# The start of an attention and feed-forward kernel: other loads, other engines and another order for the first head block

## The chip, the cores and the metric

The kernel runs on one core of a Trainium2 chip. The metric is the device time of one execution in microseconds (us); the number that counts is the median of several runs. Beside it there is one profiled execution with a trace of every instruction. In the profile PE is TensorE (PEld its weight loads), DVE is VectorE, ACT is ScalarE, POOL is GpSimd and SP is SyncE. L330 is line 330 of the kernel before.

## The reference

For 8 batches of 8 heads with 576 positions and 64 channels the kernel computes causal attention with an additive bias, and then a gated feed-forward block over the 4608 tokens of width 512 (1536 hidden channels):

```
scores = q @ k.T / 8 ;  cum = cumsum(max(s, 0))
bias   = min(-(cum[query] - cum[key]), 0)
attn   = softmax(where(key > query, -1e9, scores + bias)) ;  x = attn @ v
out    = (silu(x @ w_gate) * (x @ w_val)) @ w_out
```

q, k, v, s and the weights come as float32, the output is float32. Inside, the kernel works in bfloat16 with float32 sums.

## The kernel before, in words

**Head blocks.** The 64 heads are worked on in 16 blocks of four. For each block k and q are loaded as tiles of 128 partitions (rawk, rawq), cast to bfloat16 (ck, cq), transposed on PE against an identity (through PSUM banks) and copied from PSUM into two tiles KQ[block % 2][r], r = 0 or 1. A KQ tile holds two heads: 64 of its 128 partitions are the 64 channels of k and q, and four rows of the other 64 partitions are the bias: the running sum of s, split into a high and a low part in bfloat16, beside constant rows of about 1 and -1, so that one matmul over the partitions gives scores and bias together. For r = 0 the channels are partitions 0 to 63 and the bias rows 64 to 67, for r = 1 the bias rows are 0 to 3 and the channels 64 to 127. All other rows must be zero, because the score matmul contracts over all 128 partitions.

**Scores.** `score_piece(bh, ci)` (L352) takes a PSUM bank, adds a mask from the tile `lower` in batch 0 (L367), multiplies (L373) and lets ACT exponentiate (L383), which gives the bank back. Four pieces make a head. `av_piece` (L410) multiplies the result with v, `av_out` (L426, L427) divides.

**Banks.** There are eight PSUM banks. `take` gives the bank that was released longest ago, by the order of the program. A bank that holds transposed k or q is given back only when `pe_out` (L328 on ACT, L330 on DVE) has copied both halves r out of it.

**Order.** The order on each engine is the order of the program, written out by hand (L949 to L1032); engines wait on each other through semaphores, and each engine works strictly through its list. The trace shows that the dependencies go by region and not by tile: PE reads the high part of the sums in HL from 6.77 us on (L914), while DVE still writes the low part (L245, to 6.93 us) and the copy (L246, 6.97 to 7.77 us).

**The start.** SP loads s and then k and q of block 0 in halves r (L145, from 1.45 us). PE runs 32 idle products to raise its clock (`keep_warm`, L900). DVE sets constants, scans s (L241), and writes the high and low sums into HL (L244, L245, L246). ACT casts the halves k and q of r = 0 (L268), PE transposes them (L315), and ACT and DVE copy them out (`row_out`, `pe_out`). The bias rows of head 0 are not loaded by DMA: PE picks them with a selection matrix (`pick`, L914), and ACT and DVE scale them into KQ (`picked_row`, L925, L929). The bias rows of heads 1 to 3 come by one DMA each from HL (`aug`, L188 on SP), when all of HL is written; those of block 1 follow on the same queue. POOL makes the identity and the mask, clears rows of KQ (L226, L234), loads k and q of block 1 (L145), casts the halves r = 1 of block 0 (L270), loads v of batch 0 (L162, five DMAs), casts q of block 1 (L260), loads weights (L346) and casts v (L173). DVE copies out the halves r = 1 of block 0 (L970, L972), casts k of block 1 (L971), and copies out block 1, first the halves r = 0 (`half_batch`, L989, L992) and, after the scores of head 3, the halves r = 1 (L996 to L998). Later blocks are worked on beside the feed-forward part, which fills PE.

## Time and profile before

| what | value |
|---|---|
| median of 3 runs | 373.54 us (373.49 to 373.61) |
| the profiled execution | 373.92 us, its span 372.0 us |
| PE busy | 363.2 us (98% of the span), 3288 matmuls |
| DVE, ACT, POOL busy | 291.1, 239.9, 212.4 us |
| PE busy from 5 to 19 us | 11.87 of 14 us |
| PE busy from 19 to 27 us | 8.00 of 8 us |
| the chain that ended last, shares | PE 83%, DVE 10%, DMA 2%, ACT 2%, issue 2%, POOL 1% |

The span is the time from the first to the last instruction of the profile. The chain is the list of instructions that a step-by-step walk back from the last instruction meets, each time to what released it. A share of busy time is a mean over stages: the kernel as a whole is filled with matmuls, its first 19 us are not.

### The profile page before, as it was taken

How to read it: one execution, taken by the hardware profiler on the slowest of the kernel's cores; microseconds unless marked ns; L12 is line 12 of the kernel's file. 1: busy time of each engine (PE TensorE's matmuls, PEld its weight loads, DVE VectorE, ACT ScalarE, POOL GpSimd, SP SyncE). 2: the span in 40 equal slices, each digit the busy share in tenths (PEclk: the TensorE clock that was granted, in tenths of full speed). 3: DMA queues.
4: the chain of work that ended last, by engine and by line, in shares of the span. 5: the costliest groups of instructions: out<-in, count | busy, mean ns of one | idle time of the engine just before them, and what ended most of it. 6: DMA issues, size and time to landing. Idle time of an engine off the chain costs nothing.

```text
span 372.0 us, 8786 instructions
## 1 busy us (share of the span) xinstructions
PE 363.2 (98%) x3288; PEld 230.3 (62%) x3288; DVE 291.1 (78%) x585; ACT 239.9 (65%) x470; POOL 212.4 (57%) x325
## 2 busy tenths in 40 slices
PE   7899999999999999999999999999999999999996
PEld 6684556655555557855685558655865585476465
DVE  8978776377985899589967897699868867975984
ACT  8877776778886967688757875786565523323321
POOL 8983556955266547594749464955675516315320
PEclk9999999999999999999999999999999999999999
DMA  7999999799879996996789484994142113002003
GB/s 238 220 254 259 215 272 257 239 299 227 252 172 307 199 268 181 162 285 217 214 179 263 160 185 157 265 210 114 40 121 62 35 30 118 0 3 86 28 0 113
DMA packets 97133, 64.21 MB, mean 173 GB/s; under 512 B 77228, under 2 KB 82724, under 8 KB 97092
## 3 DMA queue, kind: packets, MB, share of 16 engines
q1 hardware_dynamic: 84964, 41.46, 46.9%
q0 software_dynamic: 12128, 22.21, 22.7%
q8 instruction: 25, 0.41, 0.5%
q14 instruction: 16, 0.13, 0.1%
HBM read 37.90 MB, written 19.86 MB: 155 GB/s over the span
## 4 chain that ended last, share of the span: by engine, by line
PE 83%; DVE 10%; DMA 2%; ACT 2%; issue 2%; POOL 1%; DVEq 0%; ACTq 0%
PE banks L643 43%; PE banks L749 17%; PE banks L373 9%; PE banks L410 7%; PE banks L700 5%; DVE kq L330 3%; DMA pk<-ks 2%; DVE pp L666 2%; DVE ht L677 1%; DVE kq L288 1%; ACT th L664 1%; POOL vt L173 1%; ACT pt L383 1%; PE banks L459 1%; PE banks L301 0%
## 5 line engine op out<-in xcount | busy, mean ns | idle before, releaser
L383 ACT ACTIVATE pt<-banks 128x512 bf16<-128x512 f32 (+1 forms) x256 | 120.4, 511 | 29.8 <-PE banks L373 17.1
L643 PE MATMUL banks<-XT,wg 128*128 128x512 bf16 x432 | 111.4, 379 | 0.4 <-DVE pp L666 0.3
L643 PE MATMUL banks<-XT,wv 128*128 128x512 bf16 x432 | 110.9, 379 | 0.1
L664 ACT ACTIVATE th<-banks 128x512 bf16<-128x512 f32 x108 | 64.7, 599 | 56.3 <-PE banks L643 51.4
L666 DVE SCALAR_TENSOR_TENSOR pp<-th,banks 128x512 bf16<-128x512 bf16 x108 | 73.7, 682 | 18.3 <-ACT th L664 18.0
L677 DVE SCALAR_TENSOR_TENSOR ht<-pp,banks 128x512 bf16<-128x512 bf16 x108 | 74.1, 687 | 10.3
L373 PE MATMUL banks<-kq 128*128 128x128 bf16 (+4 forms) x576 | 76.4, 240 | 0.8 <-DVE kq L330 0.3
L686 POOL TENSOR_TENSOR ht<-ht 128x512 bf16<-128x512 bf16 x35 | 40.4, 1154 | 53.3 <-DVE su L684 53.2
L373 PEld LDWEIGHTS <-kq 128*128 128x128 bf16 x576 | 46.1, 98 | 30.7 <-issue 2.4
L643 PEld LDWEIGHTS <-wv 128*128 128x128 bf16 x432 | 38.4, 98 | 36.2 <-issue 0.2
L643 PEld LDWEIGHTS <-wg 128*128 128x128 bf16 x432 | 38.4, 98 | 34.1 <-issue 0.7
L410 PEld LDWEIGHTS <-pt 128*128 128x128 bf16 x960 | 41.8, 98 | 17.7 <-issue 0.7
L388 POOL TENSOR_SCALAR_AFFINE_SELECT pt<-pt 128x512 bf16<-128x512 bf16 x56 | 36.6, 653 | 25.9 <-ACT pt L383 21.7
L410 PE MATMUL banks<-vt,pt 128*128 128x65 bf16 x960 | 46.8, 194 | 0.5 <-DVE ot L427 0.4
L444 POOL DMA_DIRECT2D xs<-ot x24 | 21.7, 904 | 30.4 <-DVE ot L427 28.0
L749 PEld LDWEIGHTS <-ht 128*128 128x128 bf16 x336 | 31.2, 98 | 4.3
L427 DVE TENSOR_TENSOR ot<-banks,rc 128x320 bf16<-128x320 f32 x64 | 31.5, 492 | 2.2
L188 POOL DMA_DIRECT2D kq<-HL x48 | 29.2, 610 | 0.0
L700 PE MATMUL banks<-wo,ht 128*128 128x512 bf16 x96 | 25.8, 379 | 0.0
L749 PEld LDWEIGHTS <-su 128*128 128x128 bf16 x252 | 23.6, 98 | 3.3
L814 POOL TENSOR_TENSOR ysb<-ysb 128x512 f32<-128x512 f32 x12 | 15.2, 1269 | 15.3 <-DVE ysb L808 15.3
L749 PE MATMUL banks<-WS,ht 128*128 128x256 bf16 x168 | 22.9, 273 | 0.0
(101 smaller groups left out, 377.2 us busy)
## 6 DMA issues: line engine op xcount, KB each, us to landing
out_dram<-ysb POOLq DMA_DIRECT2D x32, 256.0 KB, 4.0
rawv<-in_v_dram SPq DMA_DIRECT2D x28, 256.0 KB
rawk<-in_k_dram SPq DMA_DIRECT2D x12, 576.0 KB
rawq<-in_q_dram SPq DMA_DIRECT2D x12, 576.0 KB
xs<-ot POOLq DMA_DIRECT2D x24, 160.0 KB, 3.7
ks<-ck SPq DMA_DIRECT2D x11, 288.0 KB
qs<-cq SPq DMA_DIRECT2D x11, 288.0 KB
rawk<-in_k_dram POOLq DMA_DIRECT2D x3, 576.0 KB, 6.0
```

What stands on the lines that cost most here:

```text
L373: nc.tensor.matmul(sc[:, o : o + w], T[:, 1, e * S + 128 * tj : e * S + 128 * (tj + 1)], T[:, 0, e * S + lo : e * S + hi], start=not maske ...
L383: nc.scalar.activation(pt[:, c0 : c0 + n], sc, AF.Exp, scale=0.125)
L388: nc.gpsimd.affine_select(pt[:, 1088:1600], pt[:, 1088:1600], pattern=[[0, 4], [1, 128]], compare_op=ALU.is_ge, fill=zreg, base=0, channel ...
L410: nc.tensor.matmul(av[:, bi * (D + 1) : (bi + 1) * (D + 1)], pt[:, c0 : c0 + 128], VT[b % 2][:, tj, h, :], start=(tj == 0), stop=(tj == bi),)
L427: nc.vector.tensor_mul(ot[:, :, e * D : (e + 1) * D], av3[:, :, 0:D], rc[:, :, None].to_broadcast([128, NCH, D]),)
L643: nc.tensor.matmul(view(bs, TT), w[:, c, f0 : f0 + 128], xt[:, c, :], start=(c == 0), stop=(c == 3),)
L664: nc.scalar.activation(th, pg, AF.Tanh, scale=0.5)
L666: nc.vector.scalar_tensor_tensor(pp, in0=th, scalar=1.0, in1=pg, op0=ALU.add, op1=ALU.mult)
L677: nc.vector.scalar_tensor_tensor(hp[:, 2 * k2 : 2 * k2 + 2, :].rearrange("p a n -> p (a n)"), in0=pp, scalar=0.5, in1=pv, op0=ALU.mult, op ...
L686: (nc.vector if ft == NFT - 1 else nc.gpsimd).tensor_sub(hp[:, 1:3, :], hp[:, 1:4:2, :], hp[:, 0:3:2, :])
L700: nc.tensor.matmul(view(pys[ts_], DM), hps[ft // 2][:, 2 * (ft % 2) + half, c0 : c0 + 128], WO[j][:, ft % WKO, :], start=(ft == 0), stop=( ...
L749: nc.tensor.matmul(ps, lhs(p), rhs(p), start=(first and p == 0), stop=(last and p == NP - 1), skip_group_check=True,)
```

## The change

The parts of the change, in the order of the program:

- k and q of block 0 are no longer loaded as float32 by SP. `load_first` loads each half by a DMA from POOL that casts to bfloat16 on the way, into a layout in which each half r is contiguous. The casts on ACT (L268) and POOL (L270) are gone. The mask `lower` is made between the halves r = 0 and r = 1; the loads of block 1 follow directly.
- A tile `idle`, set to zero by DVE, takes the place of the identity in the 31 (before: 32) idle products at the start. Ten more idle products stand between the third and the fourth score piece of head 0, on a bank of their own.
- The score matmul of r = 0 uses 68 partitions instead of 128. The zeroing of the other rows of the two r = 0 tiles (DVE L222 for the columns of head 1 in the first, POOL L234 in the second) is gone; `pads` clears only the padding columns of k, and that of the second pair of tiles comes later.
- The bias rows of heads 1 to 3 come in parts: the constant row by one DMA each before the sums exist (`aug_const`), and the sums by two DMAs each (`aug_sums`) that do not need the copy of the sums (L246). That copy, now `second_copy`, comes after `picked_row(0)` on DVE, and the bias rows of block 1 after it.
- `pick` is called in the order high part for k and q, then low part for k and q.
- The copy of k of r = 1 out of PSUM goes to ACT, one half before the first exponential and one after the third. The transposes of q of r = 1 come before the first score piece on PE. DVE casts k and also q of block 1, after the copies of q of r = 1.
- On POOL, the loads of v come before the copies and transposes of the rest; the cast of q of block 1 is gone from it.

```diff
@@ -110,6 +110,7 @@
     r_m = first.tile([128, 1], FP32)
     PTP = {0: first, "bufs": 7}
     lower = first.tile([128, 512], BF16)
+    idle = first.tile([128, 128], BF16)
 
     with tc.manual_schedule():
         loaded = {}
@@ -149,6 +150,24 @@
                 ),
             )
 
+        cts = {}
+        firsts = {}
+
+        def load_first(name, r):
+            if r == 0:
+                cts[name, 0] = cp.tile(
+                    [128, J, NR, D], BF16, tag="c" + name, bufs=2, name="c" + name
+                )
+                firsts[name] = cts[name, 0].rearrange("x j r d -> x (j r d)").rearrange(
+                    "x (r j d) -> x r j d", r=NR, j=J
+                )
+            nc.gpsimd.dma_start(
+                firsts[name][:, r].rearrange("x j d -> x (j d)"),
+                SRC[name][0][0, 2 * r : 2 * r + 2, :, :].rearrange(
+                    "e (p j) d -> (e p) (j d)", j=J
+                ),
+            )
+
         def load_qk(hb):
             load_one(hb, "k")
             load_one(hb, "q")
@@ -195,22 +214,26 @@
             nc.gpsimd.memset(VT[i][:, :, :, D : D + 1], 1.0)
             nc.gpsimd.memset(VT[i][64:128, 4, :, 0:D], 0.0)
 
-        for r in range(NR):
-            load_one(0, "k", (r, r + 1))
-            load_one(0, "q", (r, r + 1))
-
-        nc.vector.memset(warm, 0.0)
-        nc.vector.memset(one_s, 1.0)
-        nc.scalar.activation(warm, warm, AF.Exp)
-        nc.vector.memset(sel, 0.0)
-        nc.vector.memset(HL[:, 0:2, 0, :].bitcast(FP32), ONES2)
-        nc.vector.memset(HL[:, 2:4, 1, :].bitcast(FP32), NEGS2)
         make_identity(nc, ident)
+        load_first("k", 0)
+        load_first("q", 0)
         nc.gpsimd.memset(lower, 0.0)
         nc.gpsimd.affine_select(
             lower, lower, pattern=[[0, 4], [1, 128]],
             compare_op=ALU.is_ge, fill=nc.gpsimd.to_reg(MASKED), base=0, channel_multiplier=-1,
         )
+        load_first("k", 1)
+        load_first("q", 1)
+        for nm in ("k", "q"):
+            load_one(1, nm, eng=nc.gpsimd)
+
+        nc.vector.memset(warm, 0.0)
+        nc.vector.memset(one_s, 1.0)
+        nc.vector.memset(idle, 0.0)
+        nc.scalar.activation(warm, warm, AF.Exp)
+        nc.vector.memset(sel, 0.0)
+        nc.vector.memset(HL[:, 0:2, 0, :].bitcast(FP32), ONES2)
+        nc.vector.memset(HL[:, 2:4, 1, :].bitcast(FP32), NEGS2)
         for lo in range(2):
             nc.vector.tensor_copy(
                 sel[:, lo, 64 + lo : 68 : 2], ident[0:BH, 0:1].to_broadcast([BH, 2])
@@ -219,11 +242,10 @@
         nc.vector.tensor_add(r_k[up], ident[up, 64:65], ident[up, 65:66])
         nc.vector.tensor_add(r_q[up], ident[up, 66:67], ident[up, 67:68])
         nc.vector.tensor_scalar_mul(r_m[up], r_q[up], -1.0)
-        nc.vector.memset(aug_rows(0, 0)[:, :, S // 2 :], 0.0)
 
         def pads(i):
             for r in range(2):
-                nc.gpsimd.memset(KQ[i][r][64 * r : 64 * r + 64, :, NR * S :], 0.0)
+                nc.gpsimd.memset(KQ[i][r][64 * r :, 1, NR * S :], 0.0)
 
         for i in range(2):
             rows = aug_rows(i, 1)
@@ -231,11 +253,7 @@
                 rows.rearrange("p a n -> p (a n)"),
                 one_s[0:64, 0:1].to_broadcast([64, NR * S + 64]), 0.0,
             )
-        nc.gpsimd.memset(aug_rows(1, 0), 0.0)
         pads(0)
-        pads(1)
-        for nm in ("k", "q"):
-            load_one(1, nm, eng=nc.gpsimd)
 
         nc.vector.tensor_scalar(s_sb, s_sb, 0.0, 8.0, ALU.max, ALU.mult)
         nc.vector.tensor_tensor_scan(
@@ -243,12 +261,25 @@
         )
         nc.vector.tensor_copy(HL[:, 0, 1, :], c8)
         nc.vector.tensor_sub(HL[:, 1, 1, :], c8, HL[:, 0, 1, :])
-        nc.vector.tensor_copy(HL[:, 2:4, 0, :], HL[:, 0:2, 1, :])
+
+        def second_copy():
+            nc.vector.tensor_copy(HL[:, 2:4, 0, :], HL[:, 0:2, 1, :])
+
+        def aug_dst(h):
+            r, e = divmod(h, 2)
+            r0 = 64 * (1 - r)
+            return KQ[0][r][r0 : r0 + 4, :, e * S : (e + 1) * S]
+
+        def aug_const(h):
+            nc.sync.dma_start(aug_dst(h)[2:4, 1, :], HL[h : h + 1, 2:4, 1, :])
+
+        def aug_sums(h):
+            rows = aug_dst(h)
+            nc.sync.dma_start(rows[0:2, :, :], HL[h : h + 1, 0:2, :, :])
+            nc.sync.dma_start(rows[2:4, 0, :], HL[h : h + 1, 0:2, 1, :])
 
         SP4 = [nc.sync] * 4
         GP4 = [nc.gpsimd] * 4
-
-        cts = {}
 
         def cast_one(hb, name, eng):
             cts[name, hb] = cp.tile([128, J, NR, D], BF16, tag="c" + name, bufs=2, name="c" + name)
@@ -259,16 +290,6 @@
             else:
                 eng.tensor_copy(dst, src_t)
 
-        def cast_half(hb, name, r, eng):
-            if r == 0:
-                cts[name, hb] = cp.tile([128, J, NR, D], BF16, tag="c" + name, bufs=2, name="c" + name)
-            dst = cts[name, hb][:, :, r, :]
-            src_t = loaded[name, hb][:, r, :, :]
-            if eng is nc.scalar:
-                nc.scalar.copy(dst, src_t)
-            else:
-                eng.tensor_copy(dst, src_t)
-
         def scratch(hb):
             for name, SC in (("k", KS), ("q", QS)):
                 nc.sync.dma_start(
@@ -310,10 +331,9 @@
                 ps = view16(bs, (j1 - j0) * 128).rearrange("p (j x) -> p j x", x=128)
                 tps[name, g] = [ps, bs, 2]
             ps = tps[name, g][0]
-            ct = cts[name, hb]
             for j in range(j0, j1):
                 nc.tensor.transpose(
-                    ps[64 * r : 64 * r + 64, j - j0, :], ct[:, j, r, :], ident
+                    ps[64 * r : 64 * r + 64, j - j0, :], firsts[name][:, r, j, :], ident
                 )
 
         def pe_out(hb, name, g, r, eng):
@@ -358,7 +378,7 @@
                 )
             pt = pts[bh]
             r, e = divmod(hh, 2)
-            T = KQ[hb % 2][r]
+            T = KQ[hb % 2][r][0 : 68 if r == 0 else 128]
             bs = take()
             n = sum(hi - lo for _, lo, hi in CHUNKS[ci])
             sc = view(bs, n)
@@ -897,7 +917,7 @@
 
         def keep_warm(n, b):
             for _ in range(n):
-                nc.tensor.matmul(view(b, 128), ident, ident, start=True, stop=True)
+                nc.tensor.matmul(view(b, 128), idle, idle, start=True, stop=True)
 
         def row_half(nm, r):
             for g in range(2):
@@ -907,15 +927,14 @@
             for g in range(2):
                 pe_out(0, nm, g, r, engs[g])
 
-        def pick(side):
+        def pick(side, lo):
             b = PICK[side]
-            for lo in range(2):
-                for c0, c1 in ((0, 512), (512, S)):
-                    nc.tensor.matmul(
-                        banks[:, b + c0 // 512, 0 : c1 - c0], sel[:, lo, :],
-                        HL[:, lo, 1, c0:c1], start=(lo == 0), stop=(lo == 1),
-                        skip_group_check=True,
-                    )
+            for c0, c1 in ((0, 512), (512, S)):
+                nc.tensor.matmul(
+                    banks[:, b + c0 // 512, 0 : c1 - c0], sel[:, lo, :],
+                    HL[:, lo, 1, c0:c1], start=(lo == 0), stop=(lo == 1),
+                    skip_group_check=True,
+                )
 
         def picked_row(side):
             b = PICK[side]
@@ -946,35 +965,41 @@
                 av_piece(h, range(NCH))
                 av_out(h)
 
-        keep_warm(32, 7)
-        cast_half(0, "k", 0, nc.scalar)
-        cast_half(0, "q", 0, nc.scalar)
-        aug(0, SP4, range(1, HB))
-        aug(1, SP4)
+        keep_warm(31, 7)
+        for h in range(1, HB):
+            aug_const(h)
+        for h in range(1, HB):
+            aug_sums(h)
+        load_v(0, range(5), nc.gpsimd)
         row_half("k", 0)
         row_out("k", 0, nc.scalar, nc.scalar)
-        cast_half(0, "k", 1, nc.gpsimd)
-        cast_half(0, "q", 1, nc.gpsimd)
-        load_v(0, range(5), nc.gpsimd)
         row_half("q", 0)
-        pick(1)
-        pick(0)
-        pe_out(0, "q", 0, 0, nc.scalar)
-        pe_out(0, "q", 1, 0, nc.vector)
+        row_out("q", 0, nc.scalar, nc.vector)
+        for lo in range(2):
+            for kq in (1, 0):
+                pick(kq, lo)
         picked_row(1)
         picked_row(0)
+        second_copy()
+        aug(1, SP4)
         row_half("k", 1)
+        pe_out(0, "k", 0, 1, nc.scalar)
+        row_half("q", 1)
         score_piece(0, 0)
         score_piece(0, 1)
-        row_half("q", 1)
-        row_out("k", 1, nc.vector, nc.vector)
-        cast_one(1, "k", nc.vector)
         row_out("q", 1, nc.vector, nc.vector)
+        for nm in ("k", "q"):
+            cast_one(1, nm, nc.vector)
         score_piece(0, 2)
+        pe_out(0, "k", 1, 1, nc.scalar)
+        b = take()
+        for _ in range(10):
+            nc.tensor.matmul(view(b, 128), idle, idle, start=True, stop=True)
+        give(b)
         score_piece(0, 3)
-        cast_one(1, "q", nc.gpsimd)
         w_load("g", 0)
         init_vt(0)
+        pads(1)
         for c in range(3):
             cast_v(0, c, nc.gpsimd)
         load_one(2, "k", eng=nc.gpsimd)
```

## The prediction

> **What bounds the kernel now.** I read first the busy time by stretches, because a share over the whole span mixes stages. Columns: stretch, its length, then for each engine busy us (instructions), the granted clock, the DMA share and GB/s.
>
> ```profile
> 9.00:11.00 2.00, 1.87 (x21) 1.20 (x20) 1.97 (x4) 1.12 (x3) 2.00 (x4) 1.00 0.94 314
> 11.00:13.00 2.00, 1.36 (x16) 0.97 (x15) 1.97 (x3) 2.00 (x6) 2.00 (x3) 1.00 0.97 244
> ...
> 17.00:19.00 2.00, 1.63 (x20) 1.11 (x19) 1.97 (x4) 2.00 (x7) 2.00 (x4) 1.00 1.15 211
> 19.00:21.00 2.00, 2.00 (x49) 1.72 (x46) 1.58 (x5) 1.82 (x5) 2.00 (x4) 1.00 1.13 304
> ...
> 200.00:300.00 100.00, 100.00 (x928) 63.55 (x926) 82.61 (x173) 66.85 (x135) 61.96 (x93) 1.00 0.57 139
> ```
>
> PE (first pair) has gaps until 19 us and hardly any from 19 us on, while DVE is full until 19 us. All of the change lies before that point. Its worth is therefore the shift of the moment at which PE becomes the bound. Next the chain of waits up to there (start, length, what):
>
> ```profile
> 8.44 0.17 DVE kq L929
> 8.61 0.63 issue
> 9.24 1.20 DVE kq L330 x2
> 10.44 0.29 issue
> 10.73 0.76 DVE ck L260
> 11.49 0.03 issue
> 11.53 1.47 DVE kq L330 x2
> ...
> 15.96 2.83 DVE kq L330 x4
> 18.79 0.04 issue
> 18.83 0.19 PE banks L367
> ```
>
> DVE works without a break from the bias rows of head 0 (8.44) to the last copy of block 1 (18.79). That copy gives back the bank for the last score piece of head 5 (18.83); from there the chain is PE. ACT is the second limit:
>
> ```profile
> 9.80 3.46 ACT L383 ACTIVATE pt<-banks 128x512 bf16<-128x512 f32 x8 [0.98 <-PE banks L373]
> 13.91 6.45 ACT L383 ACTIVATE pt<-banks 128x512 bf16<-128x512 f32 x16 [0.65 <-PE banks L373]
> 20.54 1.69 ACT L383 ACTIVATE pt<-banks 128x512 bf16<-128x512 f32 x4 [0.18 <-PE banks L373]
> ```
>
> The exponentials of heads 0 to 5 fill 9.80 to 20.36, with 0.65 idle at 13.3. After 20.36 ACT waits for PE 0.18, and before head 7 another 0.2, so ACT may be about 0.4 us later, relative to PE, than it is now.
>
> **The loads, the unknown of this change.** SP's load of the first k half was issued at 1.45 and released ACT at 4.68: 3.2 us. POOL's load of k of block 1, twice the bytes, shows
>
> ```profile
> 4.85 0.91 POOL L145 DMA_DIRECT2D rawk<-in_k_dram  x1
> 5.75 0.74 POOL L145 DMA_DIRECT2D rawq<-in_q_dram  x1
> ```
>
> and 5.3 us to landing (q: 6.0). So a half-sized casting load from POOL costs between 3.2 and 5.3 us from the start of its issue. By the trace's packet records the first packet follows 1.6 us after the start of POOL's issue against 1.3 for SP's k half; the bytes of a half are the same as SP's and its queue is empty, so I stay near that row: 3.6 us. POOL's issues take 0.9 (first) and 0.75 each. After the identity (1.38) come k at 1.4, q at 2.3, the mask (0.52 + 0.63), then the r = 1 halves, k at 4.2 and q at 4.95, and block 1 at 5.7 and 6.45. Landings: k 5.0, q 5.9, k of r = 1 7.8, q of r = 1 8.55; block 1 by its own row 5.7 + 5.3 = 11.0 and at most 6.45 + 6.0 = 12.45.
>
> A row here speaks against POOL as the issuer. Of the v loads, with 0.88 us as the median, the one that lay beside DVE's cast of k (10.73 to 11.49, SBUF to SBUF) took 1.08. The Trainium skill (DMA: Bandwidth & Descriptors, section SWDGE vs HWDGE vs iDMA) says why that can be: POOL writes its descriptors into SBUF, and DVE locks it out there in its two-port modes, which loads from SP never meet. In the changed kernel the first issue lies beside DVE's two constant fills of HL (1.20 to 2.34). By the row this costs 0.2 us on the first load; if the rule meant a full lock, up to 0.9 us on the k half, and the sum below would lose about half of its gain.
>
> **The change part by part.**
>
> *k and q of r = 0.* Removed: two ACT casts of 0.67, which put the transposes at 5.40 and 6.15. Now they start at 5.0 and 5.9: 0.4 and 0.25 earlier, with bounds from 0.8 earlier to 1.4 later (3.2 and 5.3 in place of 3.6).
>
> *The sums on DVE.* The 0.59 of zeroing before the scan is gone, a small fill (0.06 to 0.17 by the other fills) is added. s landed at 3.51 by the trace's DMA records and was first used at 3.73, so 0.2 is gained, not 0.5: HL high 5.95 instead of 6.15, low 6.7 instead of 6.93. The copy L246 (0.80) leaves the path: the copy of q starts at 6.7 instead of 7.70.
>
> *Picks.* Four matmuls take 0.5 us (eight took 1.15 with the last one's tail). q's transposes end at 6.4, the high parts at 6.9, the low parts at 7.4, plus 0.2: 7.6 instead of 7.92. ACT's three copies (1.97) run from 5.5 to 7.5. Both `picked_row` steps start at 7.6 and end at 8.4 (ACT, 0.82) and 8.5 (DVE, 0.89; before: 9.33). DVE is 0.8 ahead here.
>
> *PE's order.* Both transposes of r = 1 now stand before the first score: 8.6 to 9.1 for q's nine (0.5 plus tail). Mask and scores of the first piece take 0.65: the first exponential starts at 9.75, before: 9.80. What was gained in front of it waits here for q of r = 1.
>
> *ACT.* Two copies of 0.75 and 0.72 are added (0.66 apart when they follow each other). The first lies between 8.4 and 9.1, where ACT waits for PE anyway; without that cover it would cost 0.66. The second is on ACT's path, and takes the place of the 0.65 of idle time at 13.3, which came from the copies of r = 1 (k and q both on DVE, to 13.0). Heads 0 to 5 thus end at 9.75 + 3.46 + 0.66 + 6.45 = 20.3, before: 20.36.
>
> *DVE.* After 8.5: the copy `second_copy` 0.8 (9.3), two copies of q 1.46 (10.8), the cast of k 0.79 (11.6; landed at 11.0), the cast of q, when it lands, 0.79: 12.4 to 13.2, most likely 12.4, since in the profile of before DVE's 10.73 cast did not wait and DMA has the same bytes ahead of it. Then eight copies of 0.725: 18.2, at worst 19.0. Before: 18.79. Moved off DVE: 1.46; onto it: 0.76 for q of block 1.
>
> *What hides at nothing.* The ten idle products (0.056 apart, 0.56) stand while PE waits for ACT's banks. The score matmuls with 68 instead of 128 partitions: half of the 576; the nearest rows are the weight load with 64 partitions (94 ns) against 98 with 128, and 64 x 512 products of 380 ns against 378; bounds 0 to -1 us over all, value 0. Bias rows: nine small DMAs on SP of 0.61; three lie before 6.7, six end at 10.4; head 1's two are issued by 7.9 and land some 2 us later, before its scores (10.9). Behind them on SP stand only the rows of block 1, needed from 16 us on. The `pads` of 0.20 to 0.42 and the v loads move on POOL: v starts at 7.65 instead of 8.25, and with the casts of POOL gone (0.92 + 0.89 + 1.16) the weights are issued about 0.9 earlier.
>
> *Sum.* DVE hands back the last bank 0.6 earlier; ACT, with its 0.4 of room, allows it. From there all is PE, so I pass it on, less 0.1 for what later waits on DMA: **0.5 us**. The profiled execution would go from 373.92 to 373.4; the median, 0.38 below it, from 373.54 to **373.0**.
>
> **The rivals.**
>
> *More gain.* The loads land as SP's do (3.2): q of r = 1 at 8.15, block 1 early, the first exponential at 9.3 or, with a shorter issue (0.61, the smallest row of POOL), 8.8. DVE and ACT then both end about 1.0 earlier: 372.5; with the bounds of the 68-partition scores, 372.2. For it: an empty queue, half the bytes. Against it: the 5.3 and 6.0 of POOL's own rows.
>
> *No net change.* q of block 1 lands at 12.2 or later; DVE waits for it with eight copies behind it, and ends as before: 373.5. For it: 6.45 + 6.0 = 12.45 by the row.
>
> *Slower.* q of r = 1 lands late and everything behind it in PE's list waits, though head 0 needs nothing of it. DVE's end is its landing plus 0.7 (transposes) plus 1.46 + 1.58 + 5.8, so it decides from 9.2 us on, 4.3 us after its issue; ACT's end (landing + 1.2 + 10.57) passes its room a little earlier. By POOL's 5.3 it lands at 10.25: 1.0 us later, 374.5. A clock that is granted later would add to it: the 32 idle products of before ran 107 ns apart, and 59 apart is what the transposes show at 5.4; an idle PE from 4.4 to 5.0 may cost some of it.
>
> **How the numbers follow.** Forecast 0.40 (372.6 to 373.3), more gain 0.22, no net change 0.15, slower 0.23. The range leaves out a tenth on each side: 372.2 to 374.4. A difference of 0.2%, 0.75 us, is about what a measurement of this kernel can tell from none. Of the forecast a quarter lies beyond it, with all of the second case: faster 0.32. Of the slower case 0.17 lies beyond. The rest is within: 0.51.
>
> **What would show it.** Right: transposes at 5.0 and 5.9, `picked_row` ending at 8.5, the first exponential near 9.75 right behind q's transposes, DVE's last copy of block 1 near 18.2, and PE without gaps from there. Wrong: ACT or PE waiting on q of r = 1 after 9.2, DVE waiting on rawq of block 1 after 12.2, transposes spaced 0.1 us, or the shift at 18 us lost again before the end.

## The result and the profile after

The kernel after takes **379.15 us** (median of six runs, 377.94 to 379.50), the kernel before 374.43 (six runs: the three ahead of the prediction, at 373.49 to 373.61, and three more, at 375.25 to 377.56): ratio 1.012, 95% interval 1.0091 to 1.0149. It is slower, and outside the range of the prediction. The profiled execution took 378.90 us with a span of 376.9, 4.9 above the span of before. The kernel before itself was found between 373.3 and 378.6 us in the runs beside the experiments, so a difference of a few tenths of a per cent is read below from its interval and from the traces, not from two medians.

By stretches, in the columns that the prediction explains:

```profile
9.00:11.00 2.00, 1.37 (x20) 1.09 (x18) 1.55 (x3) 1.59 (x4) 2.00 (x3) 1.00 1.00 330
11.00:13.00 2.00, 0.00 (x0) 0.00 (x0) 0.76 (x1) 0.69 (x1) 1.90 (x4) 1.00 0.99 286
13.00:15.00 2.00, 1.15 (x9) 0.84 (x10) 0.76 (x1) 0.54 (x2) 0.66 (x3) 0.79 1.06 227
15.00:17.00 2.00, 1.78 (x17) 1.60 (x16) 0.75 (x2) 1.38 (x4) 1.23 (x2) 0.50 1.14 187
```

The first pair is PE: from 11 to 13 us it does nothing, where before it was busy for 1.36 of these 2 us. DVE, full before, is busy for 0.76. The DMA share of that stretch is 0.99: PE and, for most of it, DVE stand still, the DMA engines do not. From 15 to 17 us PE looks busy, but at a granted clock of 0.50 (the third number from the end).

The chain of work that ended last names what PE waited for:

```profile
6.22 0.75 DVE HL L263
...
7.00 6.71 DMA kq<-HL
13.71 0.14 issue
13.85 0.19 PE banks L393
...
19.65 2.82 DVE kq L350 x4
...
22.51 0.19 PE banks L387
```

The low part of the sums ends at 6.97 us (L263). SP issues head 1's bias rows at 7.00, and they land 6.7 us later. The score piece that waits for them, 68 partitions by 64 columns (L393), is the last piece of **head 0**: its fifth key tile reaches 64 columns into head 1's half of KQ, so it needs head 1's rows. PE works strictly through its list, so all behind this piece waits too. The same piece in PE's row of before and of after (in brackets: the idle time in front, and what ended it):

```profile
10.79 0.19 PE L373 MATMUL banks<-kq 128*128 128x64 bf16 x1
```

```profile
13.85 0.19 PE L393 MATMUL banks<-kq 68*128 68x64 bf16 x1 [3.48 <-DMA kq<-HL]
```

The last two steps of the chain are the ones that the prediction's chain ended with, at 18.79 and 18.83 us before: 3.68 us later now. By the starts of the feed-forward activations the shift is 3.6 at 32 us, and 4.13 at the last store, so most of it happens in this place; the rest of the 4.9 of the span lies in a few smaller waits and 0.8 us in the last stores.

DVE's row in time, and ACT's, show that DVE waited for loads as well:

```profile
12.14 0.76 DVE L291 CAST ck<-rawk 128x1152 bf16<-128x1152 f32 x1 [1.56 <-DMA rawk<-in_k_dram]
13.75 0.76 DVE L291 CAST cq<-rawq 128x1152 bf16<-128x1152 f32 x1 [0.84 <-DMA rawq<-in_q_dram]
16.25 1.45 DVE L350 COPY kq<-banks 64x640 bf16<-64x640 bf16 x2 [1.74 <-PE banks L322]
```

```profile
9.38 1.58 ACT L403 ACTIVATE pt<-banks 128x512 bf16<-128x512 f32 x3 [0.39 <-PE banks L393]
14.08 0.22 ACT L403 ACTIVATE pt<-banks 128x64 bf16<-128x64 f32 x1 [2.38 <-PE banks L393]
```

The first exponential is 0.42 us earlier than before, at 9.38. What the change gained in front is thus there, and is lost right behind it. Last, why the rows are late. In the DMA queues between 7 and 10 us of the kernel before (packets, which are the pieces of transfers that the trace records, MB, share of 16 engines)

```profile
q0 software_dynamic: 254, 1.05, 89.3%
q1 hardware_dynamic: 9, 0.01, 0.9%
```

and of the kernel after, between 7 and 12 us:

```profile
## 3 DMA queue, kind: packets, MB, share of 16 engines
q0 software_dynamic: 416, 1.47, 96.1%
```

q0 is what POOL issues, q1 what SP issues. In five microseconds 416 packets of POOL's moved, and not one of SP's, though SP had issued its rows from 7.00 on. By the trace's packet records the first moved at 12.13. Before, the rows were issued at 7.80 and moved at 9.75. And block 1's loads landed at 12.13 and 13.73 (before: 10.11 and 11.72), though POOL issued them at 5.03 and 5.78, nearly when it did before (4.85 and 5.75). Behind them POOL issued v's first load at 6.85, 1.40 earlier than before (8.25).

### The profile page after: what moved, and what is told of

It is laid out like the page before. It is cut to its first block, busy times and chain, and to the rows that moved or that the text cites. A ratio compares the mean times of both kernels' runs of the same rounds, so it can differ in the third digit from the quotient of the medians.

```text
span 376.9 us, 8767 instructions
## 1 busy us (share of the span) xinstructions
PE 362.5 (96%) x3256; PEld 231.4 (61%) x3297; DVE 290.5 (77%) x584; ACT 240.5 (64%) x470; POOL 211.0 (56%) x325
## 4 chain that ended last, share of the span: by engine, by line
PE 82%; DVE 6%; DMA 6%; issue 2%; POOL 1%; ACT 1%; SPq 0%; DVEq 0%; ACTq 0%
PE banks L663 44%; PE banks L769 17%; PE banks L393 10%; PE banks L430 7%; PE banks L720 3%; DMA XT<-xs 2%; DVE kq L350 2%; DMA kq<-HL 2%; DVE pp L686 1%; DVE ht L697 1%; DMA out_dram<-ysb 1%; PE banks L322 1%; DMA s_sb<-in_s_dram 1%; POOL vt L192 1%; PE banks L479 1%
## 5 line engine op out<-in xcount | busy, mean ns | idle before, releaser
L663 PE MATMUL banks<-XT,wv 128*128 128x512 bf16 x412 | 109.3, 379 | 1.1
L393 PE MATMUL banks<-kq 68*128 68x128 bf16 (+9 forms) x576 | 77.5, 242 | 4.4 <-DMA kq<-HL 3.5
L393 PEld LDWEIGHTS <-kq 68*128 68x128 bf16 (+1 forms) x576 | 46.7, 99 | 34.1 <-issue 5.8
L413 POOL TENSOR_SCALAR_AFFINE_SELECT pt<-pt 128x64 bf16<-128x64 bf16 x56 | 14.9, 266 | 18.2 <-ACT pt L403 18.1
L720 PE MATMUL banks<-wo,ht 128*128 128x512 bf16 x90 | 24.8, 379 | 0.3
```

The lines of the kernel that those rows point to most:

```text
L393: nc.tensor.matmul(sc[:, o : o + w], T[:, 1, e * S + 128 * tj : e * S + 128 * (tj + 1)], T[:, 0, e * S + lo : e * S + hi], start=not maske ...
L663: nc.tensor.matmul(view(bs, TT), w[:, c, f0 : f0 + 128], xt[:, c, :], start=(c == 0), stop=(c == 3),)
L720: nc.tensor.matmul(view(pys[ts_], DM), hps[ft // 2][:, 2 * (ft % 2) + half, c0 : c0 + 128], WO[j][:, ft % WKO, :], start=(ft == 0), stop=( ...
```

## The experiments

Two theories stood at first. **Theory 1**: head 1's rows wait behind block 1's loads, which POOL has queued, and the casting halves push these loads back by 2 us. **Theory 2**: the rows are slow because each head's are split into smaller transfers. Shifts are of the profiled execution against that of before; "end" is the last store. All columns but the last come from one execution of each kernel. The kernels were timed in groups, each with the kernel before beside it (median 374.04 to 375.34), so across groups the ratios compare better than the medians. Diffs are against the kernel after, if nothing else is said.

| kernel | head 1's rows move | block 1's k, q land | PE waits for them | DVE's last copy of block 1 ends | end | ratio to before, 95% |
|---|---|---|---|---|---|---|
| before | 9.75 | 10.11, 11.72 | 0 | 18.78 | 0 | 1 |
| after | 12.13 | 12.13, 13.73 | 3.48 | 22.46 | +4.13 | 1.0091 to 1.0149 |
| e1 rows in one transfer | 11.44 | 10.87, 12.97 | 3.82 | 23.73 | +4.57 | 1.0060 to 1.0153 |
| e2 before, rows split | 9.89 | 10.27, 11.91 | 0 | 19.25 | +1.22 | 0.9974 to 1.0049 |
| e3 block 1 from SP | 11.97 | 10.4, 14.0 | 2.32 | 21.98 | +3.67 | 1.0065 to 1.0170 |
| e4 70 idle products | 12.37 | 11.99, 13.60 | 0.49 | 22.29 | +3.13 | 1.0058 to 1.0106 |
| e5 before, 68 partitions | 9.34 | 9.38, 11.18 | 0 | 18.91 | -0.19 | 1.0007 to 1.0062 |
| e6 no cast loads | 10.40 | 9.51, 11.48 | 0 | 21.26 | +2.08 | 0.9975 to 1.0041 |
| e7 mask last | 10.10 | 9.51, 11.12 | 1.46 | 20.69 | +1.51 | 1.0002 to 1.0064 |
| e8 rows first | 8.29 | 11.35, 13.25 | 0 | 19.69 | +1.68 | 1.0011 to 1.0079 |
| e9 v later | 10.84 | 11.81, 13.47 | 3.07 | 21.62 | +2.45 | 0.9993 to 1.0060 |
| e10 e7, 45 idle products | 10.78 | 10.23, 11.86 | 0 | 20.41 | +2.21 | 1.0039 to 1.0096 |
| e11 e6, 37 warming products | 9.87 | 9.25, 10.80 | 0 | 19.10 | -0.02 | 0.9980 to 1.0017 |
| e12 rows before block 1's q | 8.54 | 9.60, 11.77 | 0 | 19.10 | +0.90 | 0.9991 to 1.0032 |
| e13 block 1 in halves | 10.60 | 10.39, 12.25 | 1.28 | 19.39 | +0.90 | 1.0014 to 1.0051 |
| e14 e12, v later | 8.62 | 9.56, 11.44 | 0 | 18.55 | +0.03 | 0.9991 to 1.0043 |
| e15 e7, halves | 9.90 | 9.46, 11.03 | 0.76 | 18.63 | -0.34 | 0.9970 to 1.0011 |
| e16 e15, v later | 9.79 | 9.56, 11.02 | 0.98 | 18.48 | +0.59 | 0.9985 to 1.0030 |
| e17 before, halves | 10.05 | 9.05, 11.65 | 0.31 | 19.38 | +0.68 | 0.9994 to 1.0049 |

"Head 1's rows move" is the first packet of the sums of head 1 (of all its rows, where they go by one transfer). The wait is that of PE at the last piece of head 0; in e4 and e10 the idle products cover it. One thing more changes with some of these edits: v's first load, which POOL issues behind the rest. It stands at 6.85 to 6.88 in after, e1, e4, e7 and e10, at 5.37 in e3, at 7.75 to 8.65 in e6, e8, e9, e11, e12, e13 and e15, at 9.4 to 9.5 in e14 and e16, and at 8.15 to 8.82 in the kernels made from before (e2, e5, e17). What one of these edits gained can thus be v's in part.

**e1: is the split the cause?** The rows go by one transfer per head again, the second copy right behind the sums.

```diff
-        for h in range(1, HB):
-            aug_const(h)
-        for h in range(1, HB):
-            aug_sums(h)
+        aug(0, SP4, range(1, HB))
```

> The changed kernel with the bias rows of heads 1 to 3 sent as before, one DMA of four rows per head after the copy of the sums, which stands right behind the sums again. Theory 1 (the rows wait in the DMA engines behind POOL's loads of block 1): the first row DMA is issued near 7.8 and still does not land before 13 us; PE waits about 3 us or more before the last score piece of head 0, and the time stays within 1 us of the changed kernel, near 379. Theory 2 (the split into two DMAs of few rows, on fewer DMA engines, is what is slow): the rows land 3 us after their issue, at 10.8, PE waits under 1 us, the clock stays, and the time falls by 3 to 4 us, to 375 to 376.

378.57 us (four runs, 377.42 to 379.03), a wait of 3.82. The split is not the cause: Theory 2 falls.

**e2: the split rows alone**, in the kernel before, with `second_copy` behind the picked rows as in the kernel after.

```diff
-        aug(0, SP4, range(1, HB))
+        for h in range(1, HB):
+            aug_const(h)
+        for h in range(1, HB):
+            aug_sums(h)
```

> The kernel before with only the split of the bias rows: constants early, two DMAs of sums per head, the copy of the sums after the rows of head 0. k and q of block 0 still come from SP, and block 1 from POOL at 4.9 and 5.8. Theory 1: the rows of head 1 land about 10 to 10.7, when block 1 drains, as before; no wait on PE above 0.3 us, the time within 0.5 us of before, at best 0.3 less. Theory 2: they land 6 to 7 us after their issue near 7, at 13 to 14; PE waits about 3 us, the clock falls, and the time is 3 to 4.5 us above before.

375.12 us, 0.8 above before beside it and level with it by the interval; PE doesn't wait, so Theory 2 fails here too. The rows were issued 0.85 us earlier than before (6.96) and moved at nearly the same time, 9.89, shortly before block 1's k had landed (10.27; before: 9.75 and 10.11). Issuing them early gains nothing here.

**e3: block 1 from SP**, behind the constant rows and ahead of the sums on SP's queue.

```diff
-        for nm in ("k", "q"):
-            load_one(1, nm, eng=nc.gpsimd)
...
         for h in range(1, HB):
             aug_const(h)
+        for nm in ("k", "q"):
+            load_one(1, nm)
```

> The changed kernel with k and q of block 1 loaded by SP, behind the constant rows, instead of POOL. Theory 1: the row DMAs stand behind 1.2 MB on their own queue, which drain by about 9.5 us; they land at 9.5 to 10.5 instead of 13.7, PE waits under 0.7 us, and the time falls to 373 to 375. Theory 2: the rows still need 6.7 us from their issue, PE waits 3 us, 378 to 379.

378.50 us: the gain that Theory 1 named didn't come. The bytes of block 1 ahead of the rows are the same, now on the rows' own queue, and the rows moved at 11.97. So the wait doesn't need POOL's queue. But without these two issues POOL came to v at 5.37, 1.5 us earlier than after, so v's bytes are in the way too, and the run doesn't separate the two.

**e4: the gap filled with idle products.**

```diff
-        for _ in range(10):
+        for _ in range(70):
```

> The changed kernel with 70 idle products instead of 10 before the last score piece of head 0: 60 more at 0.056 us fill 3.4 us of the wait on PE with work. The wait for the rows is the same in both theories; the kernel tells what the fall of the clock adds to it. If the clock's half speed from 14.2 to 17.6 us costs 0.6 us (the time from the end of the wait to the last copy of block 1 is 8.66 here against 8.04 before), the clock stays granted and the time falls by 0.4 to 0.7 us; if it costs nothing (ACT and DVE bound that stretch), by 0.0 to 0.2.

377.30 us (eight runs, 376.61 to 377.91), more of a gain than either expectation. PE keeps its full clock throughout, and yet DVE's last copy of block 1 ends only 0.17 earlier than after. The chain of this run shows why, the second row transfer of head 2:

```profile
9.52 7.45 DMA kq<-HL
16.97 0.04 issue
17.01 0.60 PE banks L393 x6
```

With the clock kept, PE reaches the next rows earlier and waits for those. The half clock of the kernel after follows from the wait (the rows move no earlier here, at 12.37), and it costs little at this place. At the end of the run it is 1.0 us in the profiled executions (3.13 against 4.13) and 1.85 by the medians, whose ranges don't overlap. So about 1 to 1.9 of the 4.7 us that the change lost seem to come by way of the clock; where they arise behind the last copy is not shown.

**e5: the 68 partitions alone**, in the kernel before.

```diff
-            T = KQ[hb % 2][r]
+            T = KQ[hb % 2][r][0 : 68 if r == 0 else 128]
```

(and without the clearings that this makes needless)

> The kernel before with one part of the change alone: even heads' score products take 68 partitions instead of 128, and the clearings that this makes needless are dropped (the second half of the bias rows of tile 0, the bias rows of tile 1's other half, the pads of the r=0 tiles). No load, cast or order changes. Theory 1: this part is no cause of the loss; the products take the same time per column, so the time is that of the kernel before, ratio 0.997 to 1.002, and block 1's loads, issued somewhat earlier because POOL clears less, land up to 0.5 us earlier. Rival (the narrower products are slower, or the shorter clearings move POOL's work into a worse place): 375 to 377 beside a before of about 374.5, with the last score piece of head 5 later than 18.83 us.

375.71 us: Theory 1's ratio (up to 1.002) was missed by the median, and the rival's range held, with a loss of 0.1 to 0.6% by the interval. The profiled execution (373.82 us), though, ends 0.19 earlier than that of before, with the last copy 0.13 later, so the traces show no cause for a loss. It is the fastest of the twelve, though. Five of the others, 376.65 to 378.14, had a mean granted clock of 0.986 to 0.995, the remaining seven 0.999 or more and a median of 375.23. Lost clock is thus a part of it; why these runs lost it, and the rest, stays open.

**e6: the loads of block 0 as before**, fp32 halves from SP with casts on ACT and POOL, and the pads and clearings of POOL ahead of block 1's loads.

```diff
-        load_first("k", 0)
-        load_first("q", 0)
...
+        for r in range(NR):
+            load_one(0, "k", (r, r + 1))
+            load_one(0, "q", (r, r + 1))
```

> The changed kernel with the halves of block 0 loaded by SP as float32 and cast by ACT (r = 0) and POOL (r = 1) again; all else of the change stays, and POOL issues block 1 near 4.5 us. Theory 1 (the rows of head 1 move only when the loads that POOL queued on their DMA engines have passed, and the casting halves push block 1's loads 2 us back): block 1's packets end near 10 to 11, head 1's rows move near 10 and land by 10.8, PE waits for them under 0.5 us, and the time is that of before, 373 to 374.5. Rival (the rest of the change is what costs, through ACT's two added copies or DVE's two casts): the time stays 2 us or more above before.

The wait at the last piece of head 0 is gone, and block 1 lands at 9.51 and 11.48. But the runs fall in two groups, 374.51 to 374.63 (four) and 376.09 to 376.67 (six). The profiled one (376.37) is of the upper, and in it PE is slow from the start (groups of PE up to 8.5 us; mean ns of one is the second number behind the bar):

```profile
L336 PE MATMUL banks<-ident,ck 128*64 128x128 bf16 x9 | 1.2, 314 | 0.7 <-ACT ck L977 0.7
L934 PE MATMUL banks<-HL,sel 64*128 64x512 bf16 x3 | 1.6, 609 | 0.0
```

PE is idle for 0.7 us in front of the first transposes, and was granted its clock only at 13.45.

**e11: six warming products more** to fill that gap, all else as in e6.

```diff
-        keep_warm(31, 7)
+        keep_warm(37, 7)
```

> The kernel after without the cast loads (fp32 halves from SP, casts on ScalarE and GpSimd), with 37 warming products instead of 31. With 31, the runs fell in two groups, 374.5 to 374.6 (four) and 376.1 to 376.7 (six), and in the profiled one, of the upper group, TensorE was idle for 0.7 us before the first transposes and was granted full clock only at 13.45 us. Theory 1: the groups are the moment of the grant; without the gap the clock is granted at or before 6.7 us in every run, all runs stand at 373.3 to 374.6, and the last score piece of head 5 ends at 18.5 to 19.2. Rival (the groups are of another origin, such as the loads' landings): two groups again, some 374.5 and 376.4.

374.34 us, twelve runs in one group (373.68 to 375.08), beside 374.33 for before. The clock is granted at 4.32, and the same group of PE now reads

```profile
L934 PE MATMUL banks<-HL,sel 64*128 64x512 bf16 x4 | 1.2, 377 | 0.3 <-DVE HL L264 0.3
```

The range is a little wider than Theory 1 had it (to 374.6), but the second group is gone. That the groups of e6 were the moment of the grant fits this; it isn't shown directly, since no run of the lower group has a trace. And without the cast loads, and with v's loads at 7.99 again, the rest of the change (picks by parts, ACT and DVE casts, early rows, 68 partitions) is worth nothing that can be measured, neither gain nor loss.

**e7: the mask behind the loads.** POOL issues all six loads first, so that the last four are queued about 1.2 us earlier. (The select that fills the mask moves with the clearing.)

```diff
         load_first("q", 0)
-        nc.gpsimd.memset(lower, 0.0)
...
         load_first("k", 1)
         load_first("q", 1)
         for nm in ("k", "q"):
             load_one(1, nm, eng=nc.gpsimd)
+        nc.gpsimd.memset(lower, 0.0)
```

> The changed kernel with the mask made after all six loads instead of between the halves: the halves r = 1 and block 1 are issued 1.2 us earlier, the work is the same. Theory 1: block 1's packets end 1 us earlier, the rows move near 11.1 instead of 12.1, the wait on PE falls from 3.5 to about 2.5 us, and the time by 1.0 to 1.5 us, to 377.5 to 378. Rival (the rows wait a fixed time of about 6 us after their issue): nothing changes, 378.5 to 379.

376.37 us, 2.8 below the kernel after, more than was expected. v's issue hardly moves (6.88), so this is the order of the loads alone. Block 1 lands 2.6 us earlier for an issue that is 1.2 earlier, and PE's wait becomes

```profile
12.11 0.19 PE L393 MATMUL banks<-kq 68*128 68x64 bf16 x1 [1.46 <-DMA kq<-HL]
```

**e8: the rows ahead of block 1.** POOL first copies two elements of the finished sums, and only then issues block 1's loads.

```diff
-        for nm in ("k", "q"):
-            load_one(1, nm, eng=nc.gpsimd)
...
+        nc.gpsimd.tensor_copy(marks[0:BH, :], HL[:, 1, 1, 0:2])
+        for nm in ("k", "q"):
+            load_one(1, nm, eng=nc.gpsimd)
```

> The changed kernel with POOL's loads of block 1 held back until the sums exist (one small POOL copy from HL stands ahead of them), so that SP's first row DMAs meet empty DMA queues. Theory 1: head 1's rows land by 9.5, PE does not wait for them at all, and the last piece of head 0 follows the third at once. In exchange block 1 is issued near 7.1 and lands at 12.4 and 14, DVE waits for it, and its last copy ends near 20.5: 375 to 376, so 3 us less than the changed kernel with the same work. Rival: the rows land at 13 to 14 again and the time does not fall below 378.

377.05 us, above the 375 to 376 of Theory 1, below the 378 of its rival. Head 1's first transfer of sums, issued at 7.01 with nothing of block 1 queued ahead, moves 1.3 us later, and the last piece of head 0 doesn't wait. Its second transfer, issued at 7.69, behind POOL's issue of block 1's k (7.17), moves 3.15 us later, at 10.84, and head 1's own scores wait for it:

```profile
11.47 0.82 PE L396 MATMUL banks<-kq 68*128 68x128 bf16 x8 [0.57 <-DMA kq<-HL]
```

Of two neighbouring transfers in one execution, the one with block 1 ahead of it waits 1.9 us longer. Now block 1 is late:

```profile
13.27 0.76 DVE L294 CAST cq<-rawq 128x1152 bf16<-128x1152 f32 x1 [1.14 <-DMA rawq<-in_q_dram]
14.06 5.63 DVE L353 COPY kq<-banks 64x640 bf16<-64x640 bf16 x8
```

DVE's last copy ends at 19.69, 0.9 later than before, behind its wait for q (landed at 13.25). In the kernel after q lands 0.48 later still, so of the 3.7 there block 1's own lateness is some 0.9 to 1.4, by this estimate, and the rest comes with the rows.

**e9: v's loads later**, behind two clearings of POOL that stood further down.

```diff
+        init_vt(0)
+        pads(1)
         load_v(0, range(5), nc.gpsimd)
```

> The changed kernel with POOL's two clearing steps for the v tile and the second pads moved ahead of the loads of v: v's first load is issued near 8.5 instead of 6.85 (8.25 in the kernel before), block 1 as in the changed kernel. If it is v's many small descriptors, written while block 1 is on its way, that slow block 1 down, its loads land about 1 us earlier (11 and 12.5 instead of 12.1 and 13.7), the rows with them, and the time falls by about 1 us. If v has no part in it, block 1 and the rows land as in the changed kernel and the time stays within 0.5 us of it.

376.23 us (375.44 to 377.57), 2.9 below the kernel after; the profiled execution, 377.34, is of the later ones. In it the rows moved 1.3 us earlier, PE's wait was 3.07 instead of 3.48, and block 1 landed 0.3 earlier. v's bytes, queued behind block 1, are thus a part of the loss, and by the times no small one: with v alone put back to about its old place (8.17) the interval includes the time of before. The trace shows only the smaller piece of this. The runs say more: four of the ten, the profiled one among them, had a mean granted clock of 0.992 to 0.995 and took 376.60 to 377.57, the other six 0.998 or more and 375.44 to 377.02 (median 375.57). In the kernel after all six runs had 0.991 to 0.995. So lost time and lost clock go together here.

**e10: e7 with more idle products.**

```diff
-        for _ in range(10):
+        for _ in range(45):
```

> The kernel after with the mask made after the six loads and 45 idle products instead of 10 behind the copy of the block 0 pieces, so that TensorE is idle less while it waits for head 1's rows. With the mask moved alone the time was 376.4 (1.0033) and the clock was at half from 12.79 to 16.21 us. Theory 1 (what is lost is the wait for the rows, about 1.5 us, and what the half clock adds behind it, about 0.6 to 1): the clock stays at full speed, the last score piece of head 5 comes 0.3 to 0.8 earlier than with the mask moved alone, time 375.3 to 376.0. Rival (the clock costs nothing, since VectorE's wait for block 1 sets the pace there): 376.2 to 376.6 again.

377.41 us: no gain over e7 (376.37), rather a loss. Theory 1's expectation failed; the rival had no gain, but its 376.2 to 376.6 was missed as well. The clock stayed at full speed, and DVE's last copy ended 0.28 earlier (the end, though, 0.7 later), but as in e4 the chain goes over the next rows (a transfer from 9.24 to 15.08). The rows also moved 0.7 later than in e7 (10.78), so the two don't differ by the clock alone.

**e12: the rows between block 1's k and q.** The mask stands behind the halves r = 1 and block 1's k, and its q waits for the sums as in e8.

```diff
+        load_first("k", 1)
+        load_first("q", 1)
+        load_one(1, "k", eng=nc.gpsimd)
         nc.gpsimd.memset(lower, 0.0)
...
-        load_first("k", 1)
-        load_first("q", 1)
-        for nm in ("k", "q"):
-            load_one(1, nm, eng=nc.gpsimd)
...
+        nc.gpsimd.tensor_copy(marks[0:BH, :], HL[:, 1, 1, 0:2])
+        load_one(1, "q", eng=nc.gpsimd)
```

> The kernel after with the mask made after block 1's k load, and block 1's q load held back on GpSimd until the bias sums exist (a copy of two elements from the sums ahead of it). Theory 1 (head 1's rows wait behind what GpSimd has queued, and each load of block 1 is worth about 1.5 us of that): k of block 1 lands by about 9.0, head 1's rows move by 8.3 to 9.5, TensorE doesn't wait for them at the last piece of head 0, q of block 1 lands at 11.8 to 12.5 and VectorE waits for it at most 0.5; the clock is kept; time 374.0 to 375.3, nearer to the kernel before than the 376.4 and 377.0 of its two parents. Rival (any order of the loads gives the same loss, since the bytes ahead of block 2 are what counts): 376 to 377.

375.04 us (twelve runs, 374.47 to 375.61), as expected, and level with before by its interval. Head 1's first transfer of sums moves at 8.54, 1.3 us after its issue and with most of k through (14 of its 16 completions by 8.8), the second, issued at 7.94 behind POOL's issue of q (7.41), at 11.04, 3.1 us after: the same difference as in e8. What is left are waits for this second transfer, and for the rows of heads 2 and 3, in this order:

```profile
11.84 0.82 PE L396 MATMUL banks<-kq 68*128 68x128 bf16 x8 [0.86 <-DMA kq<-HL]
13.82 0.60 PE L396 MATMUL banks<-kq 128*128 128x128 bf16 x6 [0.59 <-DMA kq<-HL]
15.80 0.82 PE L396 MATMUL banks<-kq 128*128 128x128 bf16 x8 [0.39 <-DMA kq<-HL]
```

**e13: block 1 in halves.** The same bytes at the same place of POOL's list, in four transfers of 288 KB.

```diff
         for nm in ("k", "q"):
-            load_one(1, nm, eng=nc.gpsimd)
+            for r in range(NR):
+                load_one(1, nm, (r, r + 1), eng=nc.gpsimd)
```

> The kernel after with block 1's k and q loaded in halves (four transfers of 288 KB from GpSimd instead of two of 576 KB); the bytes and their place in the queue are the same, two issues of some 0.6 us come on top. In ten of the runs so far head 1's rows first moved between 1.1 us before and 0.9 us after block 1's k had landed, and always before its q had. Theory 1a (the rows get their turn when the transfer that the DMA engines are in is through): the rows move when the first half of k is through, at 9 to 10.7 us instead of 12.1, the wait at the last piece of head 0 falls from 3.5 to 0.3 to 1.9, the time to 376.0 to 378.0. Theory 1b (the rows wait until all bytes queued at their issue, k and q, have nearly gone): the rows move at 12 to 13 again, the wait is 3 us or more, the time 378.5 to 380.

375.40 us: the ratio goes from 1.012 to 1.0032, 3.75 us by the medians. k lands at 10.39 instead of 12.13, q at 12.25 instead of 13.73, though POOL's issues take longer (1.28 and 1.07 us for the two pairs, against 0.78 and 0.76). Because of that v's first load is issued 1.0 us later as well (7.85), and e9 has shown that this counts: how much of the gain is the halves' and how much is v's is not separated. The wait is

```profile
11.66 0.19 PE L394 MATMUL banks<-kq 68*128 68x64 bf16 x1 [1.28 <-DMA kq<-HL]
```

1b falls: the rows moved at 10.60, before q's halves (11.38 and 12.25). 1a holds for the rows and the wait, but the time is below its 376.0 to 378.0, and it doesn't hold as it was put: the rows did not go when k's first half was through (9.08), but behind its second.

**e14: e12 with v later.**

```diff
+        init_vt(0)
+        pads(1)
         load_v(0, range(5), nc.gpsimd)
```

> The kernel with q of block 1 behind the bias sums, and v's loads 1 us later (the two clearings on GpSimd ahead of them). Its parent lost 0.9 us in its profile, with waits of TensorE of 0.86, 0.59 and 0.39 for rows of heads 2 and 3, which were issued from 8.4 us on, beside v's and q's packets. Theory 1: with v later the waits fall together by 0.5 to 1.2, q of block 1 lands no later than 11.8, and the time is 373.6 to 374.8. Rival (these waits are SyncE's own: six small transfers issued one after another at 0.6 each): the waits stay within 0.3 of 1.8 and the time at 374.6 to 375.4.

The waits for rows fell from 1.8 to 0.5 (what is left is that for head 1's second transfer) and the end came 0.87 earlier (+0.03), as Theory 1 had it. So most of these waits came from v's packets and not from SP's issues. The time, 375.26 (374.09 to 377.85), is not measurably below e12's; there the expectation failed.

**e15: both e7 and e13**, mask last and halves.

```diff
         load_first("q", 1)
         for nm in ("k", "q"):
-            load_one(1, nm, eng=nc.gpsimd)
+            for r in range(NR):
+                load_one(1, nm, (r, r + 1), eng=nc.gpsimd)
+        nc.gpsimd.memset(lower, 0.0)
```

> The kernel after with the mask behind the loads and block 1 in halves. Theory 1a: each of the two takes its part of the rows' wait; the rows move by 8.3 to 9.5, TensorE waits less than 0.4 at the last piece of head 0, block 1 has landed by 11.6, the last copy of block 1 ends at 18.6 to 19.3 and the time is 373.6 to 375.2. Theory 1b: as with the mask alone, rows from 10.1 on, a wait of about 1.5, time 376.0 to 376.8.

374.32 us (twelve runs, 373.71 to 375.33) beside 374.65 for before: level with it, with the end 0.34 earlier in the profiled execution (374.10). The rows moved later than 1a said (9.90) and PE still waited 0.76, so 1a is not the whole rule. DVE works without a break again:

```profile
9.88 1.46 DVE L351 COPY kq<-banks 64x640 bf16<-64x640 bf16 x2
11.37 0.76 DVE L292 CAST ck<-rawk 128x1152 bf16<-128x1152 f32 x1
12.04 0.92 DVE L292 CAST cq<-rawq 128x1152 bf16<-128x1152 f32 x1
12.99 5.64 DVE L351 COPY kq<-banks 64x640 bf16<-64x640 bf16 x8
```

**e16: e15 with v later.**

```diff
+        init_vt(0)
+        pads(1)
         load_v(0, range(5), nc.gpsimd)
```

> The kernel of the run before (mask behind the loads, block 1 in halves) with v's loads 1 us later, behind two clearings on GpSimd. Theory 1a: the rows of heads 2 and 3, which come behind v's packets, wait 0.3 to 0.8 us less; time 0.2 to 0.8 below the run before, 373.2 to 374.8, so level with the kernel before or better. Rival (those rows are set by SyncE's issues): the same as the run before within 0.2.

374.91 us, no better than e15, against the 0.2 to 0.8 us expected: the waits for the rows fell from 1.6 to 1.0, but DVE now waits 1.34 us for v at 19.8. The gain was handed on to another wait.

**e17: the halves in the kernel before**, the control.

```diff
         pads(1)
         for nm in ("k", "q"):
-            load_one(1, nm, eng=nc.gpsimd)
+            for r in range(NR):
+                load_one(1, nm, (r, r + 1), eng=nc.gpsimd)
```

> The kernel before with block 1's k and q loaded in halves, everything else as it was. It tells whether the halves are a gain in themselves or only take back what the change had lost. Theory 1 (in the kernel before the rows are there 0.04 us ahead of their use and VectorE waits for no load, so earlier rows and loads find nothing to shorten): ratio 0.998 to 1.002, the last copy of block 1 at 18.6 to 19.0. Rival (the halves are worth something wherever they stand): 0.5 us or more below the kernel before, ratio below 0.998.

374.67 us beside 374.04, ratio 1.0021 (0.9994 to 1.0049); the last copy at 19.38, later than Theory 1 said, behind a wait of 0.84 for PE. The rows moved at 10.05 instead of 9.75, and PE now waits 0.31 for them at the last piece of head 0. The halves are no gain in themselves: with v's delay they take back what the change had lost. No version that was run is measurably faster than the kernel before.

## Why the prediction was wrong

**The step that failed** is the one under "What hides at nothing": that head 1's rows "are issued by 7.9 and land some 2 us later, before its scores (10.9)". They were issued by 7.68; the first of the two landed 6.7 us after its issue, and was used at 13.85. The use was named wrongly too: the first one is the last piece of head 0 (10.79 before), not head 1's scores. I took the 2 us from the kernel before, where the rows moved at 9.75 and landed at 10.74, 0.04 before their use. That was no latency of the transfer alone, but the time until block 1's k was nearly through (10.11): e2 shows it, where rows issued 0.85 earlier moved no earlier, and e8, where the transfer with nothing ahead moved after 1.3 us and the one behind block 1's k after 3.15. A wait that lies 0.04 us under its cover was costed at nothing, and no price was given for the case that the cover goes.

**Block 1's loads** were mis-sized too. The prediction gave them the time of their own row, 5.3 and 6.0 us from issue, because "DMA has the same bytes ahead of it". They took 7.1 and 7.95. The rival "no net change" had q at 12.2 or later as its condition; it came at 13.73. By e8 this alone is worth at least 0.9 us at DVE's last copy, so that rival too was priced too low: it left out that rows stand behind these loads. **v's loads** were put at nothing beside the rows, with a start at 7.65; POOL came to them at 6.85, and e9 shows that their earlier start is a part of the loss.

**The loads of block 0** were right: 4.96, 5.68, 7.23 and 7.99 against 5.0, 5.9, 7.8 and 8.55. POOL's issues took 0.56 instead of 0.75. The price for a lock-out of POOL by DVE's constant fills did not show: the first issue, beside the fills, took 0.69, 0.13 above the next. So the slower rival, q of r = 1 after 9.2, did not happen.

**The steps in front** were nearly right: low sums 6.97 (6.7, so the 0.2 us that was to be gained there didn't come), `picked_row` ends 8.36 and 8.60 (8.4, 8.5), first exponential 9.38 (9.75, with q of r = 1 earlier than forecast).

**The clock** was a remark on the slower rival, for the stretch from 4.4 to 5.0. There it was granted early (3.94), and lost at 14.18 to 17.59, behind the long wait. By e4 this is a follower of the wait, not its cause, and worth about 1 to 1.9 us of the loss there, though in e10 a kept clock gained nothing; the sum had no term for it. In e6 the stretch that the prediction named seems to have cost some 1.9 us, the distance of its groups.

**The sum**, 0.5 us for the parts that were worked out, is not refuted: with the loads put right, e15's profiled execution ends 0.34 earlier than before. But no time resolves it.

Shown, then: the loss is the rows' wait behind block 1's loads (e8, e12: the first transfer of sums moves after 1.3 us, the next one, behind k or q, after 3.1), with the clock that falls behind it (e4). These loads and the rows are late by the order of what POOL queues (e7) and by v's early loads (e9); halves help together with a later v (e13, e15), and without the cast loads and with v later the loss is gone (e6, e11). What the cast loads cost by themselves is not separated. Not shown is by which rule the rows get their turn. The Trainium skill (DMA: Bandwidth & Descriptors, section Queues, rings and completion order) says that a DMA engine turns between the queues that have work, and drains a whole packet of typically 9 to 17 descriptors before it switches. Where whole loads were queued ahead of them, the rows moved within about 1 us of k's landing and always before q's (in e3, on one queue with them, 1.5 after k). This would fit if one load were one such turn; in e13 two smaller transfers went ahead of them, which would not. Here the measurement decides, and the rule stays open.

## What to carry to other kernels

A small transfer that is needed soon can be as late as the large ones queued ahead of it, on its own queue or another: read from the packet records when it first moved, not only when it landed, and ask what was in the DMA engines then. A wait that ends just before its use has a price, even if the profile shows none: work out what comes if the cover goes by a microsecond. Where big loads must stand ahead of small rows, cut them and issue them early, or hold the later ones back until the rows are out. Here this took back a loss; it made no kernel faster than the one before.

## What was not expected of the hardware

- **Size of a transfer.** 1.15 MB in two transfers landed at 12.13 and 13.73, in four, with v's loads 1.0 us later, at 10.39 and 12.25. The trace records 16 completions for a load; in the kernel after 15 of k's had come by 11.01, and one at 12.13; e13's second half of k came within 9.37 to 10.39. So one or a few parts of the load lagged there (from k's first completion to its last it took 2.1 to 3.0 us in after, e1, e4 and e9, 1.6 to 1.7 in e2 and e10, and 0.9 to 1.5 in before, e6, e7, e11 and e12). Why is not known.
- **Full stop of the other queue.** From 6.7 to 12.1 us no packet of SP's queue moved beside POOL's, though rows were issued from 7.00 on. It is no rule for all loads: the constant rows, on the same queue, had moved between 4.9 and 6.7, while the casting loads of r = 1 (landed at 7.23 and 7.99) were under way.
- **The clock.** In the profiled runs it was granted at 3.94 to 6.69 us, in e6 at 13.45, and after PE had waited 3.48 us it was halved for 3.41; in e1, from 13.41 on, within the wait of 3.82 that ended at 14.52, for 6.83; e7 and e9 lost it for 3.41 behind waits of 1.46 and 3.07, while e3 kept it through one of 2.32. The granted stretches before the loss were 10.24 (after, e9) and 6.83 (e1, e7), all multiples of 3.41. The Trainium skill (TensorE: Matmul & The Clock Gate, section What's actually happening) states a free-running window of 3413 ns: these rows agree with its length.
